# One head group's transposes moved from TensorE to a DMA, and a hold on loads released earlier

## The chip, the cores and the metric

The kernel runs on one core of one Trainium2 chip. The core has five engines that run side by side, each through its own queue in order: TensorE (PE, matrix multiplies; PEld is its loading of weights), VectorE (DVE), ScalarE (ACT), GpSimd (POOL) and SyncE (SP). In this kernel POOL issues the loads, and SP issues DMA transposes and stores. Sixteen DMA engines move the data; the profile calls the queue that POOL feeds q0 and the one that SP feeds q1. The metric is the time of one execution on the device in microseconds.

## The reference

Two steps, in f32 at the interface. The kernel computes in f16 with f32 sums.

```python
scores = scale * np.matmul(q, k.transpose(0, 1, 3, 2)) - np.log(S)
attn = 1.0 / (1.0 + np.exp(-scores))
attn_out = np.matmul(attn, v)
x = attn_out.transpose(0, 2, 1, 3).reshape(B * S, H * D)
out = (np.maximum(x @ w_gate, 0.0) * (x @ w_val)) @ w_out
```

q, k and v are 8 batches x 12 heads x 448 positions x 64 wide. x is 3584 x 768; w_gate and w_val are 768 x 1536, w_out is 1536 x 768. The attention has a sigmoid in place of a softmax, so no sums over rows are needed.

## The kernel before

**Attention.** The 12 heads of a batch are worked on in three head groups of four (`NG = 3`). For a group, q and k have to stand with the head dimension on the partitions: that is the tile `qkT` of (batch, group), which has three buffers. It can be made in two ways. `pe_transposes(b, g, ti)` lets TensorE multiply 14 blocks of k (`ti` 0) or q (`ti` 1) with an identity into a PSUM bank (`trt`, L204), and VectorE copies the bank to `qkT` (L211). `dma_transposes(b, g)` lets VectorE regroup k and q into a tile `rel` with two buffers (L222), and SP issues one DMA that transposes all of it into `qkT` (L226). `both(b, g)` is the two `pe_transposes` of a group. `qk_unit(b, g, c)` then computes the scores of one of seven chunks of keys (L239) and the sigmoid on ScalarE (L187, tile `PT`), and `pv_group(b, g)` multiplies with v (L257) and puts the result into `xT` (L184).

**The gated layer.** Its 1536 columns are 12 chunks f. `gv` computes gate and value of a chunk (L322, tiles `g_ps` and `v_ps`), the relu on ScalarE or VectorE, and their product into `hT` (L343). Batch 0 is split into two halves of its queries (256 and 192), so it has 24 such units, which wait in `gv_queue`. Later batches use a scheme with fewer multiplies on sums of tiles (L400, L714), whose sums VectorE makes (L391, L584), among them sums `T` of the weight `wo`.

**Order.** All of it is one order written out by hand; each engine's queue follows it. Batch 0's attention comes first. Then, for batch 1, six bursts of `qk_unit` (units 0 to 2, 3 to 5, 6 to 8, 9 to 12, 13 to 16, 17 to 20 of the 21 of a batch) alternate with `ffn_mix`, which takes 4, 3, 3, 3, 3 and 4 units from `gv_queue`. `hooks` puts further work into a mix: the pair (3, job) runs the job when 3 units of the mix are left, so with a mix of 3 ahead of them all. Unit 6 is the last of group 0; group 1 begins with unit 7, the second of the third burst.

**Loads.** POOL issues them in the order written, k and q a head group at a time (`load`), w_gate and w_val a few chunks at a time (`load_gv`), v of a batch in three transfers (`load_v`). It has eight completion semaphores for them, so an issue waits for the landing of the one eight places before it. `load(2, ...)` reuses batch 0's tiles. `late_loads`, in the last mix of batch 1, issues the DMA transpose of batch 2's third group and then `hold(2, 2)`: a tiny copy on POOL that reads that `qkT`, and so keeps POOL from issuing v of batch 2, k and q of batch 3, `wo` and v of batch 3 until that transpose has landed.

**PSUM.** After batch 0 eight banks go round in a ring (`bank`); who takes a bank waits for the reader of what it held eight takes earlier.

Of the kernel before, what the change touches and what calls it, by code (L numbers as in the profile page):

```python
# [18 lines left out]
def kernel(  # L19
# [75 lines left out]
    def tiles_of(b):  # L95
        if b not in in_tiles:
            pool = early if b == 1 else inp
            in_tiles[b] = tuple(
                p.tile([P, NPAIR, NCH * D], FP16, tag=t, name=t)
                for p, t in ((pool, "k16"), (pool, "q16"), (vinp, "v16"))  # L100
            )
        return in_tiles[b]

    def rows_of(src, b):
        return src[b].rearrange("(x r) (t c) d -> (r t) x (c d)", r=2, c=NCH)

    def load(b, g0, g1, which, c0=0, c1=NCH):
        for nm, t16, src in zip("kq", tiles_of(b), (k, q)):
            if nm in which:
                xs, cs = slice(2 * g0, 2 * g1), slice(c0 * D, c1 * D)  # L110
                nc.gpsimd.dma_start(t16[:, xs, cs], rows_of(src, b)[:, xs, cs])  # L111

    def load_v(b):
        v16 = tiles_of(b)[2]
        nc.gpsimd.dma_start(v16[:, 0::2, :], rows_of(v, b)[:, 0::2, :])
        for r in range(2):
            nc.gpsimd.dma_start(
                v16[64 - 64 * r : P - 64 * r, 1::2, :], rows_of(v, b)[64 * r : 64 * r + 64, 1::2, :]
            )
# [25 lines left out]
    def load_gv(f0, f1, which=(0, 1)):  # L145
        fs = slice(f0 * P, f1 * P)
        for i in which:
            wt, src = ((wg, moe_w_gate), (wv, moe_w_val))[i]
            nc.gpsimd.dma_start(wt[:, :, fs], src[:, fs].rearrange("(c p) f -> p c f", p=P))  # L149
# [2 lines left out]
    load_gv(0, 2)  # L152
    load_gv(2, 4)
    load(1, 0, 1, "kq")
    load_gv(4, 6)
    load(1, 1, 2, "kq")
    load_gv(6, 9)
    load_v(1)
    load(1, 2, 3, "kq")
# [30 lines left out]
    def qkT_of(b, g):  # L190
        if (b, g) not in qkT_tiles:
            qkT_tiles[(b, g)] = qkTp.tile([P, TW, P], FP16, tag="qkT", name="qkT")
        return qkT_tiles[(b, g)]

    def pe_transposes(b, g, ti, c0=0, c1=NCH):
        transposed(b, g, ti, c0, c1)()
# [21 lines left out]
    def dma_transposes(b, g):  # L218
        k16, q16, _ = in_tiles[b]
        rel = relp.tile([P, TW, P], FP16, tag="rel", name="rel")  # L220
        for ti, t16 in enumerate((k16, q16)):
            nc.vector.tensor_copy(  # L222
                rel[:, ti * NCH : (ti + 1) * NCH, :].rearrange("p c (h d) -> p h c d", h=2),
                t16[:, 2 * g : 2 * g + 2, :].rearrange("p h (c d) -> p h c d", c=NCH),
            )
        nc.sync.dma_start_transpose(  # L226
            qkT_of(b, g)[:], rel[:].rearrange("p c x -> p (c x)")
        )
# [78 lines left out]
    def pv_group(b, g):  # L307
        pv(b, g, 0, S, [PT_tiles.pop((b, g, c))[:, :, 0:S] for c in range(NCH)])
# [453 lines left out]
    def push_gv(b, q0, qn, fs, act_relu=True):  # L762
        for f in fs:
            gv_queue.append(lambda f=f: gv(b, q0, qn, f, act_relu))

    def push_first(half, fs, act_relu=True):
        c0, c1 = HALVES[half]
        push_gv(0, 64 * c0, 64 * (c1 - c0), fs, act_relu)
# [16 lines left out]
    half = QCUT // 2 * D  # L785
# [60 lines left out]
    slots[5].pv()  # L846
    push_first(1, range(0, 4))
    for f0 in range(4, 12, 2):
        for half in range(2):
            for f in range(f0, f0 + 2):  # L850
                push_first(half, (f,), (half, f) not in ((0, 9), (1, 8)))


    order = [(g, c) for g in range(NG) for c in range(NCH)]
# [1 line left out]
    def pv_finish(b):  # L856
        pv_group(b, NG - 1)
# [4 lines left out]
    def hold(b, g):  # L862
        nc.gpsimd.tensor_copy(gate[0:1, :], qkT_tiles[(b, g)][0:1, 0, 0:2])

    def both(b, g):
        pe_transposes(b, g, 0)
        pe_transposes(b, g, 1)

    def late_loads():
        dma_transposes(2, 2)  # L870
        hold(2, 2)
        load_v(2)
        load(3, 0, NG, "kq")
        load_o()
# [57 lines left out]
    for b in range(1, B):  # L932
        if b == 1:
            cuts, pv_at = (0, 3, 6, 9, 13, 17, 21), {3: (0, 2), 5: (1, 2)}
        else:
            cuts, pv_at = (0, 4, 7, 11, 14, 18, 21), {0: (-1, 2), 2: (0, 2), 4: (1, 2)}
        bursts = list(range(len(cuts) - 1))
        inner = {}
        if b > 2:
            inner = {0: 1, 3: 5} if b == 3 else {0: 1} if b % 2 == 0 else {2: 3, 3: 5} if b == B - 1 else {4: 5}  # L940
            for n in inner.values():
                bursts.remove(n)
        count = len(bursts)
        hooks = {}
        if b == 1:
            mix = (4, 3, 3, 3, 3, 4)
            hooks = {
                1: [(3, lambda: both(1, 1))],
                3: [(3, lambda: both(1, 2))],
                4: [(3, lambda: dma_transposes(2, 0)), (1, lambda: dma_transposes(2, 1))],  # L950
                5: [(4, late_loads)],
            }
            steps = itertools.chain.from_iterable(early_sum_steps(j, 2 * j) for j in range(4))
            given = ((0, 0, 1, 1, 1), (0, 1, 1, 0), (0, 1, 1, 1), (0, 1, 1, 0), (2, 0, 0, 0), (0, 1, 1, 1, 1))
        else:
            mix = (0,) * count

        def burst(n):
            for i, (g, c) in enumerate(order[cuts[n] : cuts[n + 1]]):
                if n in pv_at and i == pv_at[n][1]:  # L960
                    if n == 0:
                        pv_finish(b - 1)
                        if b == 2:
                            push_group(0)
                        elif b % 2 == 0:
                            push_group(b // 2 - 1)
                    else:
                        pv_group(b, pv_at[n][0])
                qk_unit(b, g, c)

        for m in range(count):
            jobs, ahead = [], []
            burst(bursts[m])
            if m == 0 and b > 3:
                jobs.append(lambda: dma_transposes(b, 2))
            if b == 2 and m == 2:
                ahead.append(lambda: dma_transposes(3, 0))
            elif b == 2 and m == 3:
                jobs.append(lambda: dma_transposes(3, 1))
            elif b == 3 and m == count - 1:  # L980
                jobs.append(lambda: dma_transposes(4, 1))
            elif 0 <= m - count + 2 and 3 < b < B - 1:
                jobs.append(lambda: dma_transposes(b + 1, m - count + 2))
            if b == 1:
                if m == 0:
                    load(2, 0, 1, "kq")
                    load(2, 1, 2, "kq")
                    load(2, 2, 3, "kq")
            elif m == 0 and b + 1 < B:
                for g0, g1 in ((0, 1), (1, NG)) if b == 3 else ((0, NG),) if b > 3 else ():  # L990
                    jobs.append(lambda g0=g0, g1=g1: load(b + 1, g0, g1, "kq"))
                jobs.append(lambda: load_v(b + 1))
            if b == 2 and m == 0:
                ahead.append(lambda: split_sums(1))
            elif b == 2 and m == 4:
                open_late()
                first_sums = token_sum_steps(0, 0)
                ahead += [*first_sums[:2], lambda: weight_sums(0)]
            elif b == 2 and m == 5:
                ahead += [lambda: weight_sums(1), lambda: dma_transposes(3, 2)]  # L1000
                jobs += first_sums[2:]
            elif b == 3 and m == 0:
                jobs.append(lambda: (weight_sums(2), weight_sums(3)))
            elif b == 3 and m < 3:
                jobs.append(lambda: gate_sums(6 + 2 * m, 8 + 2 * m))
            if b % 2 and b > 2:
                if m == count - 1:
                    jobs.append(lambda: (batch_sums_t1(b // 2), batch_sums(b // 2, (0, 1))))
            elif b > 3 and m == 0:
                jobs.append(lambda: batch_sums(b // 2 - 1, (1, HD)))  # L1010
            if mix[m]:
                for job in jobs:
                    job()
                ffn_mix(mix[m], hooks.get(m, ()), steps, given[m])
            else:
                next_work(
                    jobs, ahead=ahead,
                    amid=(lambda: burst(inner[m])) if m in inner else None,
                )
            if b == 3 and m == count - 2:  # L1020
                dma_transposes(4, 0)
# [35 lines left out]
```

## Time and profile before

| what | value |
|---|---|
| median of 3 runs | 389.93 us (389.64 to 390.08) |
| the profiled execution | 390.18 us |
| its span in the trace | 388.3 us |
| TensorE busy | 381.8 us, 98% |
| VectorE, ScalarE, POOL busy | 300.0, 227.3 and 49.8 us |
| idle stretches of TensorE over 0.2 us after its first 10 us | 0.27 us at 23.56, 0.46 us at 95.07 |
| load queue q0 | 30496 packets, 23.24 MB |
| SP's queue q1 | 37664 packets, 19.24 MB |

Where a row starts with two numbers, they are start and length in microseconds from the start of the span; then come engine, line, operation, the tile written and the tiles read, the shape, and how many instructions the row stands for. In square brackets stands how long the engine was idle before it, and what ended that. In the DMA view a row names a transfer, the queue, how many there were and the time from issue to landing.

Some places in time that the change touches: POOL issued k and q of batch 1's second group at 16.91 and 18.91, and they landed at 30.89 and 32.02; w_gate and w_val of chunks 4 and 5 went out at 14.50 and 15.32. The hold ran at 62.72, the first transfer behind it was issued at 63.20, and the two parts of `wo` landed at 85.42 and 93.11.

### The profile page before, as it was taken

How to read it: one execution, taken by the hardware profiler on the slowest of the kernel's cores; microseconds unless marked ns; L12 is line 12 of the kernel's file. 1: busy time of each engine (PE TensorE's matmuls, PEld its weight loads, DVE VectorE, ACT ScalarE, POOL GpSimd, SP SyncE). 2: the span in 40 equal slices, each digit the busy share in tenths (PEclk: the TensorE clock that was granted, in tenths of full speed). 3: DMA queues.
4: the chain of work that ended last, by engine and by line, in shares of the span. 5: the costliest groups of instructions: out<-in, count | busy, mean ns of one | idle time of the engine just before them, and what ended most of it. 6: DMA issues, size and time to landing. Idle time of an engine off the chain costs nothing.

```text
span 388.3 us, 8972 instructions
## 1 busy us (share of the span) xinstructions
PE 381.8 (98%) x3576; PEld 224.0 (58%) x3576; DVE 300.0 (77%) x595; ACT 227.3 (59%) x480; POOL 49.8 (13%) x73
## 2 busy tenths in 40 slices
PE   8999999999999999999999999999999999999995
PEld 6678776884555545454455554545455555555663
DVE  3455668768777799999757789999987788999553
ACT  5967887567797755555537864545477344333321
POOL 8633305300400300003000300000000000000000
PEclk9999999999999999999999999999999999999999
DMA  9999997999997990227945793222012220000336
GB/s 172 198 200 204 204 205 114 206 194 170 136 247 141 161 224 6 48 49 95 166 89 129 139 233 54 45 52 50 0 38 67 72 72 1 2 0 2 81 82 165
DMA packets 68987, 43.81 MB, mean 113 GB/s; under 512 B 35664, under 2 KB 65616, under 8 KB 68944
## 3 DMA queue, kind: packets, MB, share of 16 engines
q0 software_dynamic: 30496, 23.24, 39.9%
q1 hardware_dynamic: 37664, 19.24, 24.2%
q10 hardware_dynamic: 784, 0.75, 0.6%
q8 instruction: 28, 0.46, 0.5%
q14 instruction: 15, 0.12, 0.1%
HBM read 47.19 MB, written 11.01 MB: 150 GB/s over the span
## 4 chain that ended last, share of the span: by engine, by line
PE 83%; DMA 10%; POOL 3%; issue 1%; DVE 1%; ACT 0%; POOLq 0%; DVEq 0%; ACTq 0%
PE u L400 34%; PE g L400 16%; PE y L400 11%; PE qk_ps L239 7%; PE pv_ps L257 7%; DMA wo<-in_moe_w_out_dram 6%; PE v_ps L322 4%; DMA wv<-in_moe_w_val_dram 3%; PE g_ps L322 3%; PE ya L366 1%; POOL q L111 1%; PE yb L366 1%; PE trt L204 1%; POOL k L111 1%; POOL wg L149 0%
## 5 line engine op out<-in xcount | busy, mean ns | idle before, releaser
L187 ACT ACTIVATE PT<-qk_ps 128x448 f16<-128x448 f32 (+3 forms) x318 | 151.0, 586 | 81.2 <-PE qk_ps L239 80.9
L400 PEld LDWEIGHTS <-S 128*128 128x128 f16 x558 | 54.6, 98 | 44.7
L633 DVE TENSOR_TENSOR gsb<-g,gsb 128x448 f32<-128x448 f32 x72 | 42.8, 624 | 10.1 <-PE g L400 9.5
L239 PE MATMUL qk_ps<-qkT 64*64 64x448 f16 (+2 forms) x756 | 47.4, 336 | 0.5 <-ACT PT L187 0.3
L400 PEld LDWEIGHTS <-hT 128*128 128x128 f16 x306 | 28.5, 98 | 22.7 <-issue 5.2
L629 ACT COPY gsb<-u 128x448 f32<-128x448 f32 x48 | 25.6, 558 | 24.0 <-PE u L400 22.9
L257 PE MATMUL pv_ps<-PT,v 64*64 64x448 f16 (+2 forms) x756 | 36.8, 329 | 0.0
L184 DVE TENSOR_SCALAR xT<-pv_ps 128x448 f16<-128x448 f32 (+2 forms) x53 | 27.8, 566 | 9.9 <-PE pv_ps L257 8.5
L458 ACT ACTIVATE ysb<-u 128x384 f32<-128x384 f32 x30 | 14.7, 490 | 33.9 <-PE u L400 29.0
L400 PEld LDWEIGHTS <-wg 128*128 128x128 f16 x216 | 20.2, 98 | 21.8 <-issue 4.3
L400 PEld LDWEIGHTS <-wv 128*128 128x128 f16 x216 | 21.1, 98 | 19.7
L476 DVE SCALAR_TENSOR_TENSOR ysb<-y,ysb 128x384 f32<-128x384 f32 x29 | 16.1, 556 | 17.9 <-PE y L400 10.8
L239 PEld LDWEIGHTS <-qkT 64*64 64x64 f16 x756 | 17.8, 105 | 20.5 <-issue 14.3
L111 POOL DMA_DIRECT2D k<-in_k_dram x14 | 10.8, 775 | 140.3 <-DVE rel L222 135.2
L257 PEld LDWEIGHTS <-v 64*64 64x64 f16 x756 | 21.8, 107 | 10.9 <-issue 0.9
L400 PE MATMUL u<-T,hT 128*128 128x384 f16 x132 | 25.1, 327 | 0.0
L400 PE MATMUL u<-xT,wg 128*128 128x448 f16 x108 | 23.5, 354 | 0.0
L322 PE MATMUL v_ps<-xT,wv 128*128 128x256 f16 (+2 forms) x168 | 22.8, 273 | 0.7 <-DVE hT L343 0.5
L400 PE MATMUL g<-xT,wg 128*128 128x448 f16 x108 | 23.4, 352 | 0.0
L400 PE MATMUL u<-X,wv 128*128 128x448 f16 x108 | 23.4, 352 | 0.0
L400 PE MATMUL u<-X,S 128*128 128x448 f16 x108 | 23.4, 352 | 0.0
L400 PE MATMUL g<-X,S 128*128 128x448 f16 x108 | 23.4, 352 | 0.0
(94 smaller groups left out, 563.9 us busy)
## 6 DMA issues: line engine op xcount, KB each, us to landing
out_dram<-ysb SPq DMA_DIRECT2D x52, 192.0 KB, 2.9
v<-in_v_dram POOLq DMA_DIRECT2D x8, 336.0 KB, 15.1
v<-in_v_dram POOLq DMA_DIRECT2D x16, 168.0 KB, 14.8
k<-in_k_dram POOLq DMA_DIRECT2D x4, 672.0 KB, 10.9
q<-in_q_dram POOLq DMA_DIRECT2D x4, 672.0 KB, 13.9
k<-in_k_dram POOLq DMA_DIRECT2D x9, 224.0 KB, 12.0
q<-in_q_dram POOLq DMA_DIRECT2D x7, 224.0 KB, 12.3
wo<-in_moe_w_out_dram POOLq DMA_DIRECT2D x1, 1536.0 KB, 18.5
```

Source lines behind the costliest of these rows:

```text
L111: nc.gpsimd.dma_start(t16[:, xs, cs], rows_of(src, b)[:, xs, cs])
L184: nc.vector.tensor_scalar(out=xT, in0=src, scalar1=XSCALE, scalar2=None, op0=AOP.mult)
L187: nc.scalar.activation(PT_ap, ps_ap, AF.Sigmoid, bias=sig_bias, scale=qk_scale)
L239: nc.tensor.matmul(out_of(hh)[o : o + 64, :], qkT[rows, c, cols], qkT[rows, NCH + c0 : NCH + c1, cols], start=True, stop=True, tile_positi ...
L257: nc.tensor.matmul(ps[hh][64 * r : 64 * r + 64, 0:qn], v16[rows, 2 * g + hh, c * D : (c + 1) * D], pieces[c][rows, hh, :], start=(c == 0), ...
L322: nc.tensor.matmul(ps[:, 0:qn], (wg, wv)[i][:, dc, f * P : (f + 1) * P], xT_tiles[b][:, dc, q0 : q0 + qn], start=(dc == 0), stop=(dc == ND ...
L366: nc.tensor.matmul(ps[:, 0 : m1 - m0], hT_tiles[g][:, f, t * P : (t + 1) * P], wo[:, f, m0:m1], start=(f == 0), stop=(f == NFC - 1),)
L400: nc.tensor.matmul(ps[:, 0:n], A[:, k_, :], W[:, k_, :], start=(first and k_ == 0), stop=(k_ == kn - 1), skip_group_check=True,)
L458: nc.scalar.activation(o, ps[:, 0:HM], AF.Copy, scale=OUT_SCALE)
L476: nc.vector.scalar_tensor_tensor(out=o, in0=ps[:, 0:HM], scalar=OUT_SCALE, in1=o, op0=AOP.mult, op1=AOP.add)
L629: by(gs[u][i][:], ps[u][:, 0:S])
L633: nc.vector.tensor_tensor(out=gs[u][i][:], in0=ps[u][:, 0:S], in1=gs[u][i][:], op=AOP.add)
```

## The change

It has four parts. (1) k and q of batch 1's second group are loaded before chunks 4 and 5 of w_gate and w_val instead of after. (2) That group's `qkT` is made by `dma_transposes(1, 1)` ahead of the first mix of batch 1, instead of by TensorE ahead of the second mix. (3) Of the units of chunks 8 to 11, those of chunks 8 and 9 are taken chunk by chunk (8 of both halves, 9 of both) and not half by half; chunks 10 and 11 come as before. (4) POOL's hold in `late_loads` reads `qkT` of batch 2's second group, not of its third.

```diff
     load_gv(2, 4)
     load(1, 0, 1, "kq")
+    load(1, 1, 2, "kq")
     load_gv(4, 6)
-    load(1, 1, 2, "kq")
     load_gv(6, 9)
...
     for f0 in range(4, 12, 2):
-        for half in range(2):
-            for f in range(f0, f0 + 2):
-                push_first(half, (f,), (half, f) not in ((0, 9), (1, 8)))
+        units = [(half, f) for half in range(2) for f in range(f0, f0 + 2)]
+        for half, f in sorted(units, key=lambda u: u[1]) if f0 == 8 else units:
+            push_first(half, (f,), (half, f) not in ((0, 9), (1, 8)))
...
         dma_transposes(2, 2)
-        hold(2, 2)
+        hold(2, 1)
         load_v(2)
...
             hooks = {
-                1: [(3, lambda: both(1, 1))],
+                0: [(4, lambda: dma_transposes(1, 1))],
                 3: [(3, lambda: both(1, 2))],
```

## The prediction

> **What bounds the kernel now.** I read the page first: shares, then the chain.
>
> ```profile
> PE 381.8 (98%) x3576; PEld 224.0 (58%) x3576; DVE 300.0 (77%) x595; ACT 227.3 (59%) x480; POOL 49.8 (13%) x73
> PE 83%; DMA 10%; POOL 3%; issue 1%; DVE 1%; ACT 0%; POOLq 0%; DVEq 0%; ACTq 0%
> DMA  9999997999997990227945793222012220000336
> ```
>
> TensorE is busy for 98% of the span, so a microsecond taken from it is gained, and one in which it waits is lost up to the end: there is no later slack to absorb it. The DMA digits (9.7 us each) show the transfers saturated for the first 58 us; that is where the change works. Next, the timeline of TensorE and VectorE (start, length, operation), around the work that goes and the work that needs its result:
>
> ```profile
> 34.33 0.58 PE L204 MATMUL trt<-ident,k 128*64 128x128 f16 x14
> 34.74 0.56 PE L204 MATMUL trt<-ident,q 128*64 128x128 f16 x14
> ...
> 38.95 0.76 PE L239 MATMUL qk_ps<-qkT 64*64 64x448 f16 x12
> ...
> 93.13 1.36 DVE L391 TENSOR_TENSOR T<-wo 128x2304 f16<-128x2304 f16 x1 [0.95 <-DMA wo<-in_moe_w_out_dram]
> ...
> 95.07 1.29 PE L322 MATMUL v_ps<-xT,wv 128*128 128x448 f16 x6 [0.46 <-DVE hT L343]
> ```
>
> The 28 transposes run from 34.40 to 35.30 on the chain of waits (0.90 us). The burst at 38.95 has three units of four; the first still belongs to group 0, the second, at 39.2, is the first that reads group 1. At 93.13 VectorE waited 0.95 us for wo, and TensorE 0.46 us behind that: its longest idle stretch after the start. Last, the DMA view: what one DMA transpose costs, issue to landing, each in a window around its issue (199.4, 177.5 and 78.4), and under the last the packets of two stretches after that issue (queue, packets, MB):
>
> ```profile
> qkT<-rel SPq DMA_TRANSPOSE x1, 3.9
> ...
> qkT<-rel SPq DMA_TRANSPOSE x1, 10.6
> ...
> qkT<-rel SPq DMA_TRANSPOSE x1, 14.1
> ...
> q0 software_dynamic: 609, 0.62, 124.4%
> ...
> q0 software_dynamic: 949, 0.49, 87.8%
> q1 hardware_dynamic: 947, 0.24, 45.8%
> ```
>
> Idle engines: 3.9 us. With loads issued at the same moment: 10.6. Behind loads already queued: 14.1. From 79 to 82 queue 0 (the loads) moved 609 packets and the transpose none; from 84 to 88 both moved one packet for one (949, 947). A transpose is 128x14x128 f16 in packets of 256 B, 1792 of them, so one for one is slow.
>
> **The change, part by part.** Sums go against the profiled execution (390.18 us; span 388.3 and 1.88 around it). The median of the runs is 389.93, 0.25 less.
>
> *Transposes off TensorE:* -0.90 (above). The two VectorE copies qkT<-trt (618 ns each) go, two rel copies (385 ns) come. They stand behind the xT copies that end at 29.73, in a 2.62 us idle stretch of VectorE ending at 32.34: 0, if their loads are there. Two PSUM banks fewer are taken in the ring, so the next v_ps takes the bank that the hT copy frees at 34.43; TensorE wants it at 35.06: 0.
>
> *Loads sooner:* the load queue lands strictly in order, k or q of one group each 1.12 us after the one before (30.89, 32.02), wg and wv 2.0 us. q of batch 1's first group lands at 25.78 (12.86 + 12.9). So k and q of the second come at 26.9 and 28.0, before the copies at 29.73. wg and wv of chunks 4 and 5 go from 27.78 and 29.77 to 30.0 and 32.0; TensorE wants them at 34.3 and 35.0: 0. POOL issues as many transfers as before; later ones keep their places.
>
> *The DMA transpose:* copies end at 30.42; SP has nothing ahead of it (its next transpose came at 52.04) and issues 0.1 us behind: 30.5. Behind it on SP stands only that next one, and the rel buffer is free again long before the copies at 54.4 want it: 0. TensorE reaches the second unit at 39.2 - 0.9 = 38.3. The latency decides. From below 3.9 (idle engines), from above 15.7 (the transpose issued at 82.83, partly behind another). Nearest is 78.36: then loads for over 10 us were queued, as at 30.5 (the last of them land at 41 and later), while the 10.6 had next to none ahead of it. At 78.36 the first packets came after 3.8 us, and a store issued at 105.95 behind queued loads also took 5.3 us instead of 2.9. From 30 to 34 the load queue moves 1056 packets in 4 us, 264 a microsecond; sharing one for one, by the 4 us above and the 529 and 529 packets from 92 to 95, I count 175 to 195 transpose packets a microsecond here. So 3.3 to 3.8 us until the first packet, 1792 / 185 = 9.7, and 0.4 from the last packet to the landing (62.2 to 62.66 for the third transpose): 13.4 to 13.9, the row 14.1. I take 13.9: it lands at 44.4, and TensorE stands for 6.1 us: +6.1. Ends: none (34.4), or 46.2, +7.9. Behind the waiting multiply on TensorE's queue stands everything; ScalarE and VectorE run dry, DMA gains.
>
> *Loads behind it:* 0.46 MB more at 200 GB/s put them 2.3 us later (v 41.2 to 43.5, k and q of the third group 43.5 to 45.8, wv of chunks 9 to 11 49.3 to 51.6). They are wanted at 43.0, 45.1 and 51.5 plus the stall: 0 while the stall lasts; without it up to 0.65.
>
> *Chunk 8 ahead of 9:* the same matmuls on the same engines, chunk 9 one unit (1 us) later: 0.
>
> *The stall's second price:* TensorE's clock. The table by stretch (busy time and count by engine, PEclk third from the right) at both ends of the trace:
>
> ```profile
> 0.00:5.00 5.00, 3.84 (x26) 3.32 (x28) 0.94 (x3) 1.89 (x3) 4.26 (x11) 1.00 0.62 165
> 384.40:387.00 2.60, 0.00 (x0) 0.00 (x0) 0.34 (x1) 0.00 (x0) 0.00 (x0) 1.00 0.79 222
> 387.00:388.30 1.30, 0.00 (x0) 0.00 (x0) 0.00 (x0) 0.00 (x0) 0.00 (x0) 0.60 0.00 0
> ```
>
> The last matmul ends at 384.4, and within 387.0 to 388.3 the granted clock falls (mean 0.60: 0.5 from about 387.25), 2.9 us on. At the start the clock column has no record yet, but 22 matmuls of 194 columns took 3.74 us, 0.88 ns a column, where a row of six of 448 columns takes 1.14 us, 0.42: half speed for 3.7 us, 1.9 us lost. A wait of 6.1 us is twice what let the clock fall at the end, so I take the start's price: +1.9. Ends: 0, and 2.6 if the slow stretch lasts 5 us. The Trainium skill (TensorE: Matmul & The Clock Gate, What's actually happening) has the clock halved after one idle window of about 3.4 us and back after as long a busy one; that speaks against this change too, and by it the term would be 1.7 and the time 396.4; the trace's tail fell sooner, after 2.9 us.
>
> *hold on the second transpose:* before, (2,1) landed at 59.4 and (2,2) at 62.66, and POOL went on at 62.72. Now v of batch 2, k and q of batch 3 and wo are issued 3.2 us sooner against TensorE's place; the third transpose shares engines with them, but is first read at 88.0, 25 us on: 0. wo lands some 3 us sooner than 93.11, which covers the 0.95 us of VectorE's wait: -0.46. Ends: 0 and -0.46. Late next: nothing; that g and v pair then runs back to back.
>
> Sum: 390.18 - 0.90 + 6.1 + 1.9 - 0.46 = 396.8; less 0.25, 396.6.
>
> **Rivals.**
> *The wait without the clock (394.7):* a clock that stays up through one wait. For: no wait inside the trace shows it. Against: the tail.
> *Half the contention (391.2):* latency 10.4 as at 127.79, landing 40.9, wait 2.6: 390.18 - 1.36 + 2.6 - 0.25. For: four of the eighteen transposes took 9 to 11 us. Against: they were issued together with the first loads, not behind a full queue.
> *No wait (389.2, the other side):* the transpose takes about the 3.9 us of idle engines, landing 34.4; then -0.90 - 0.46 + 0.65 for the later loads. It decides at landing 39.7 (38.3 + 1.36), a latency of 9.2. For: 52.04, queued behind four loads, took 5.8. Against: those four were the last, their stream running out 3 us on; at 30.5 it runs 25 us more. The Trainium skill (DMA: Bandwidth & Descriptors, Latency and other measured facts) gives a DMA transpose 261 GB/s; with that page's fixed 2 us this would be an estimated 3.8 us and the time 389.2; rows under load speak against it.
>
> **How the numbers follow.** Wait and clock 0.64 (395 to 398.8 by latency and clock ends), wait alone 0.14, half the contention 0.11, no wait 0.11. The forecast is the first case's 396.6. Leaving out the last case and the edges of the others, 391.0 to 398.8 holds 8 in 10. About 0.2% (0.8 us) is what can be told from no change: no wait splits into faster 0.05 and same 0.06; slower 0.89.
>
> **What would show it.** In the changed profile: 28 matmuls of L204 gone near 34; an SP transpose at 30.5 landing near 44; a wait of TensorE at L239 on DMA qkT<-rel of 6 us, then a stretch with granted clock 0.5; POOL past its hold 3 us sooner against TensorE; no wait on wo. A landing before 39 makes the prediction wrong.

## The result, and the profile after

The changed kernel takes 399.85 us, the median of 5 runs (398.39 to 400.06), against 389.93 us for the kernel before (389.64 to 390.27, 5 runs). The ratio is 1.0242, with a 95% interval of 1.0229 to 1.0254. Of all the runs told of here one stands apart and is in no number below: a run of the unused transpose with batch 2's transposes later took 563.56 us at a mean granted clock of 0.656, where the others of that kernel took about 393 at 1.0. The forecast of 396.6 us has the right sign, but it is 3.2 us short, and the time lies 1.05 us above the upper edge of its range. The profiled execution took 399.64 us, its span 397.6 us.

Busy time by engine and the granted clock in 40 slices, from the page of the changed kernel:

```profile
PE 383.5 (96%) x3548; PEld 224.7 (57%) x3548; DVE 299.6 (75%) x595; ACT 227.4 (57%) x480; POOL 50.2 (13%) x73
PEclk9999599999999999999999999999999999999999
```

28 matmuls are gone (3548 for 3576), yet TensorE is busy 1.7 us longer and the span is 9.3 us longer. The one slice in which the clock is low says where to look, from about 40 to 50 us. The timeline of TensorE there (start, length, operation, and in brackets the idle time before it with what ended that):

```profile
38.12 0.38 PE L239 MATMUL qk_ps<-qkT 64*64 64x448 f16 x4
46.72 0.96 PE L239 MATMUL qk_ps<-qkT 64*64 64x448 f16 x8 [8.21 <-DMA qkT<-rel]
47.61 1.14 PE L322 MATMUL g_ps<-xT,wg 128*128 128x192 f16 x6
```

The burst of three units breaks off after its first (4 matmuls). TensorE stands for 8.21 us until the DMA has made `qkT` of group 1, and the g_ps work after it takes 1.14 us where the kernel before needed 0.67. The table by stretch (busy time and count of PE, PEld, DVE, ACT and POOL, then the granted clock, the DMA share and GB/s) shows both prices:

```profile
40.90:46.70 5.80, 0.00 (x0) 0.00 (x0) 0.00 (x0) 0.00 (x0) 2.51 (x5) 0.50 1.30 183
46.70:51.10 4.40, 4.38 (x28) 3.16 (x29) 0.82 (x2) 2.15 (x6) 1.27 (x2) 0.50 1.31 204
51.10:55.00 3.90, 3.90 (x62) 2.72 (x60) 1.84 (x5) 2.26 (x6) 0.00 (x0) 1.00 1.27 203
```

In the first stretch no engine but POOL, which issues loads, does anything; in the second TensorE works at clock 0.50; in the third it is at full clock again.

I matched each matmul of the kernel before with the same one after and followed the difference of their start times:

| place (time before) | after minus before | step | forecast |
|---|---|---|---|
| up to 34 us | +0.09 | +0.09, the start phase | 0 |
| matmul behind the transposes that went, 35.23 | -0.83 | -0.92 | -0.90 |
| unit 7 of batch 1, 39.16 | +7.55 | +8.38, the wait | +6.1 |
| end of the slow clock, 53.0 | +9.60 | +2.05, the clock | +1.9 |
| v_ps at 95.07 | +9.03 | -0.57, no wait on wo | -0.46 |
| last matmul, 384.35 | +9.03 | 0 | 0 |

The last matmul thus comes 9.03 us later. The tail of the span behind it and the time around the span grew by 0.23 and 0.19 us; together that is 9.45 of the 9.46 us between the two profiled executions. Every step came with the forecast sign, and one has the wrong size: the wait.

The DMA view of the changed kernel says why. The first line is the transpose (issue to landing, from a window at its issue); then come the packets of both queues from 35 to 37, from 38.2 to 39.0, and from 34.4 to 46.2 us:

```profile
qkT<-rel SPq DMA_TRANSPOSE x1, 16.2
...
q0 software_dynamic: 372, 0.29, 90.1%
q1 hardware_dynamic: 373, 0.10, 35.7%
...
q1 hardware_dynamic: 33, 0.01, 94.5%
q0 software_dynamic: 24, 0.02, 63.8%
...
q0 software_dynamic: 1921, 1.57, 92.0%
q1 hardware_dynamic: 1822, 0.46, 38.8%
```

And the load queue of the kernel before over the same stretch, 34.4 to 46.2 us, with no transpose beside it:

```profile
q0 software_dynamic: 2987, 2.37, 128.2%
```

The transpose was issued at 30.50 us, as forecast, and landed at 46.67: 16.18 us in place of 13.9. Its first packet moved at 34.46, 3.96 us after the issue. Then both queues moved packet for packet (372 and 373 in 2 us), until 46.17. In 38.2 to 39.0, and once more about 43.3 to 43.7, both nearly stood still (33 and 24 packets in 0.8 us, where some 140 each would have gone). The kernel before has such a still stretch too, within the transpose of 78.36 on which the forecast rested. Its packets from 88.8 to 89.6, loads and transpose:

```profile
q0 software_dynamic: 18, 0.01, 31.6%
q1 hardware_dynamic: 21, 0.01, 29.8%
```

While the transpose of the changed kernel moved its 0.46 MB, the loads lost 2.37 - 1.57 = 0.80 MB, 4.0 us of their stream (2.37 MB in 11.8 us is 201 GB/s). That second price is hidden under the wait here, and shows below.

### The profile page after: what moved, and what is told of

It is laid out like the page before. It is cut to its first block, busy times and chain, and to the rows that moved or that the text cites. A ratio compares the mean times of both kernels' runs of the same rounds, so it can differ in the third digit from the quotient of the medians.

```text
span 397.6 us, 8919 instructions
## 1 busy us (share of the span) xinstructions
PE 383.5 (96%) x3548; PEld 224.7 (57%) x3548; DVE 299.6 (75%) x595; ACT 227.4 (57%) x480; POOL 50.2 (13%) x73
## 4 chain that ended last, share of the span: by engine, by line
PE 92%; DMA 4%; ACT 2%; DVE 1%; issue 0%; DVEq 0%; ACTq 0%
PE u L400 33%; PE g L400 15%; PE y L400 10%; PE qk_ps L239 9%; PE pv_ps L257 8%; PE g_ps L322 4%; DMA qkT<-rel 4%; PE v_ps L322 4%; PE u L714 2%; ACT PT L187 2%; PE g L714 2%; PE warm_ps L175 1%; PE ya L366 1%; PE yb L366 1%; PE trt L204 1%
## 5 line engine op out<-in xcount | busy, mean ns | idle before, releaser
L239 PE MATMUL qk_ps<-qkT 64*64 64x448 f16 (+2 forms) x756 | 48.2, 339 | 8.7 <-DMA qkT<-rel 8.2
L257 PE MATMUL pv_ps<-PT,v 64*64 64x448 f16 (+2 forms) x756 | 36.7, 329 | 0.0
L343 DVE TENSOR_TENSOR hT<-gate_sb,v_ps 128x256 f16<-128x256 f32 (+2 forms) x28 | 11.7, 419 | 21.6 <-PE v_ps L322 16.0
L322 PE MATMUL g_ps<-xT,wg 128*128 128x256 f16 (+2 forms) x168 | 24.0, 283 | 0.0
## 6 DMA issues: line engine op xcount, KB each, us to landing
v<-in_v_dram POOLq DMA_DIRECT2D x16, 168.0 KB, 15.7
```

The source lines that it names most:

```text
L239: nc.tensor.matmul(out_of(hh)[o : o + 64, :], qkT[rows, c, cols], qkT[rows, NCH + c0 : NCH + c1, cols], start=True, stop=True, tile_positi ...
L257: nc.tensor.matmul(ps[hh][64 * r : 64 * r + 64, 0:qn], v16[rows, 2 * g + hh, c * D : (c + 1) * D], pieces[c][rows, hh, :], start=(c == 0), ...
L322: nc.tensor.matmul(ps[:, 0:qn], (wg, wv)[i][:, dc, f * P : (f + 1) * P], xT_tiles[b][:, dc, q0 : q0 + qn], start=(dc == 0), stop=(dc == ND ...
L343: nc.vector.tensor_tensor(out=hT_tiles[g][:, f, o : o + qn], in0=gate_sb[:, 0:qn], in1=ps[1][:, 0:qn], op=AOP.mult,)
```

## The experiments

The theory: the whole loss is one wait for a transpose that shares the DMA engines with queued loads, and the clock that falls in the wait; the other three parts of the change are harmless. The rivals: the reordered loads or the earlier hold cost something themselves; the clock is no price of its own; the latency belongs to the transpose and not to its neighbours.

### The hold alone

The kernel before with one line changed.

```diff
-        hold(2, 2)
+        hold(2, 1)
```

> The kernel before with the hold moved alone (POOL released by the second transpose of batch 2). Theory: wo is issued 3 us sooner, VectorE no longer waits for it near 93, and TensorE's wait of 0.46 us near 95 goes: 389.5 us. Rival: the third transpose and the loads now share the engines and something behind it comes late: 389.9 or more, with a new wait of TensorE between 62 and 100.

Measured: 389.53 us (389.23 to 390.39, 11 runs) beside 390.17 for before; ratio 0.9991 (0.9982 to 1.0001). The timeline of TensorE near the place where it waited 0.46 us:

```profile
93.18 1.31 PE L322 MATMUL g_ps<-xT,wg 128*128 128x448 f16 x6
94.33 1.30 PE L322 MATMUL v_ps<-xT,wv 128*128 128x448 f16 x6
```

No bracket any more: the g and v matmuls run back to back. The wait is gone in the trace, as forecast; in the time the gain sits at the edge of what can be told.

### All but the DMA transpose

The changed kernel with group 1's transposes back on TensorE; loads, order and hold stay changed.

```diff
-                0: [(4, lambda: dma_transposes(1, 1))],
+                1: [(3, lambda: both(1, 1))],
```

> The changed kernel with the one group's transposes back on TensorE, at their old place; the three other parts of the change stay. Theory: the order of the loads and of chunks 8 and 9 costs nothing, so it equals the kernel with the hold moved alone: 389.5 us, and the whole loss of 10 us belongs to the DMA transpose. Rival: a part of the loss comes from the loads of chunks 4 and 5 that stand later, or from the order of the chunks: over 390.5 us.

Measured: 389.37 us (389.04 to 390.06, 11 runs); ratio 0.9983 (0.9974 to 0.9992). TensorE has no idle stretch over 0.2 us after the first 20 us, and the clock stays at 1.0 to its last matmul. So the three other parts together cost nothing, and this version is faster than both kernels, by 0.17% over before. All of the loss belongs to the DMA transpose in its place.

### The wait without the clock

The changed kernel with 42 matmuls of zeros, whose result nobody reads, ahead of the unit that waits.

```diff
+                if (b, n, i) == (1, 2, 1):
+                    keep_warm(42)
```

> The changed kernel with 42 multiplies of zeros (448 columns, about 8 us in all) on TensorE just ahead of the unit that waits for the DMA transpose, so that TensorE is busy while it would wait. Theory: the wait itself is unchanged (the transpose lands near 46.7), but the granted clock stays at full speed and the work behind the wait runs at its old pace: 2.1 us less than the changed kernel, 397.7 us. Rival: the slow work behind the wait comes from readers of PSUM banks or late loads and not from the clock: 399.8 us with the same slow stretch.

Measured: 397.26 us (396.78 to 397.90); ratio 1.0188 (1.0172 to 1.0204). The timeline of TensorE:

```profile
38.41 8.12 PE L175 MATMUL warm_ps<-zeros 128*128 128x448 f16 x42
46.76 0.57 PE L239 MATMUL qk_ps<-qkT 64*64 64x448 f16 x8 [0.23 <-DMA qkT<-rel]
```

And the stretch of the zeros in the table (busy time and count by engine, granted clock third from the right):

```profile
38.50:46.70 8.20, 8.03 (x42) 3.93 (x41) 0.60 (x2) 0.98 (x2) 2.84 (x4) 1.00 1.19 172
```

The unit starts at 46.76, as in the changed kernel (46.72), at clock 1.00, and takes 0.57 us instead of 0.96. The ratio falls by 0.0054, 2.1 us of 390 (1.3 to 2.9 by the two intervals): the price of the clock, by taking it away, against 2.05 us in the trace and 1.9 forecast.

### The keys alone by DMA

Half the transpose: the keys' 7 blocks (896 packets) by DMA, the queries by TensorE one mix later.

```diff
-                0: [(4, lambda: dma_transposes(1, 1))],
+                0: [(4, keys_by_dma)],
+                1: [(3, lambda: pe_transposes(1, 1, 1))],
```

> The changed kernel with only the keys of that group through the DMA transpose (half the size, 896 packets) and the queries transposed by TensorE at the old place. Theory (about 4 us behind the queued loads, then one packet for one): 4 + 896 / 165 + 0.5 = 10 us from an issue at 30.2, landing near 40.1; TensorE comes to it at 38.75 and waits 1.4 us, too short for the clock to fall: 389.93 - 0.45 - 0.46 + 1.4 = 390.4 us. Rival: the latency does not depend on the size (a fixed delay of some 16 us behind the queue): landing near 46, a wait of over 7 us, about 399 us.

Measured: 394.23 us (392.57 to 396.14, 4 runs); ratio 1.0111 (1.0078 to 1.0143). My 390.4 was wrong. The transpose in the DMA view (issue to landing):

```profile
qkT<-rel SPq DMA_TRANSPOSE x1, 11.4
```

The wait behind it, on the timeline of TensorE:

```profile
41.84 0.96 PE L239 MATMUL qk_ps<-qkT 64*64 64x448 f16 x8 [2.78 <-DMA qkT<-rel]
```

And the table over the slow stretch:

```profile
41.00:47.80 6.80, 5.96 (x35) 4.28 (x36) 1.12 (x3) 2.46 (x6) 3.59 (x5) 0.50 1.30 202
```

Halving the packets took 4.8 us off the latency (16.2 to 11.4), which is 5.4 us for each 1000 packets, the still stretches counted in, and leaves some 6.5 us that the halving doesn't touch. The wait came out at 2.78 us, 1.4 above what I expected, and it let the clock fall, which I had ruled out. Here the clock costs more than in the changed kernel, although the wait is a third: the slow stretch is 6.83 us, and only 0.83 of it lies under the wait. A slow stretch costs half of the time that TensorE works in it: (6.83 - 0.83) / 2 = 3.0 us here, against (10.24 - 5.84) / 2 = 2.2 in the changed kernel. The spread of the runs fits: the mean granted clock was 0.997 in the fastest and 0.990 in the slowest, which is the profiled one.

### A transpose nobody waits for

The version with TensorE's transposes again, plus the same two `rel` copies and the same DMA transpose at the same time, into a tile that nobody reads before it is loaded anew.

```diff
-                0: [(4, lambda: dma_transposes(1, 1))],
+                0: [(4, unused_transpose)],
+                1: [(3, lambda: both(1, 1))],
```

> The changed kernel with the group's transposes back on TensorE, and the same two VectorE copies and the same DMA transpose issued at the same time into a tile that nobody reads until it is loaded anew (extra work; nothing is left out). It measures the transfer by itself. Theory: the transpose takes 14 to 16 us again and pushes the loads behind it by about 3 us, but TensorE waits only for those loads, by 1.5 us at most: 389.5 to 391 us. Rival: the cost of the change is in the displaced loads or the extra work on VectorE and not in TensorE's wait for the result: well over 392 us.

Measured: 393.95 us (393.83 to 394.30); ratio 1.0098 (1.0080 to 1.0116): 3.8 us lost, although no instruction waits for the transpose. I had expected 391 at most; the rival's time came. The two extra copies on VectorE are not it: up to 43.9 us TensorE keeps within 0.3 us of the version without the transpose. The timeline, TensorE and VectorE:

```profile
45.29 1.51 PE L257 MATMUL pv_ps<-PT,v 64*64 64x448 f16 x25 [0.63 <-DMA v<-in_v_dram]
...
54.52 0.39 DVE L222 COPY rel<-k 128x896 f16<-128x896 f16 x1 [2.39 <-DMA k<-in_k_dram]
55.67 0.39 DVE L222 COPY rel<-q 128x896 f16<-128x896 f16 x1 [0.76 <-DMA q<-in_q_dram]
...
56.92 0.35 DVE L336 TENSOR_SCALAR gate_sb<-g_ps 128x192 f32<-128x192 f32 x1
...
57.32 0.84 PE L239 MATMUL qk_ps<-qkT 64*64 64x448 f16 x4 [1.00 <-DVE gate_sb L336]
```

The same two copies in the version without the transpose:

```profile
50.85 0.39 DVE L222 COPY rel<-k 128x896 f16<-128x896 f16 x1 [0.24 <-DMA k<-in_k_dram]
51.95 0.39 DVE L222 COPY rel<-q 128x896 f16<-128x896 f16 x1 [0.70 <-DMA q<-in_q_dram]
```

The loads behind the transpose land some 4 us later. TensorE then loses about 1.2 us waiting for v of batch 1 itself, and about 2.6 us through VectorE: its two copies for batch 2's first group wait in order for k and q, and the relu of a chunk (`gate_sb`), which is ready to go, stands behind them. So the displaced loads have a price of their own, about 3.8 us, which the wait of the changed kernel hides.

### The transpose with the queue empty

The changed kernel with all loads behind chunks 4 and 5 of w_gate and w_val held until the transpose has landed (the loads of batch 2's k and q, which stand later in the program, are moved along).

```diff
-    load_gv(6, 9)
-    load_v(1)
-    load(1, 2, 3, "kq")
-    load_gv(9, 12)
...
-                0: [(4, lambda: dma_transposes(1, 1))],
+                0: [(4, transpose_then_load)],
```

> The changed kernel with all loads behind chunks 4 and 5 held on POOL until this DMA transpose has landed, so that it runs with the load queue running empty near 31.7. The time is no measure here, since the held loads come 5 to 8 us late. Theory: the latency is contention with queued loads, so it falls to 4 to 5.5 us, landing near 35, and TensorE does not wait at that unit; it waits later, for chunks 6 to 8, some 5 us. Rival: this transpose is slow in itself or for being the first one of the execution: latency of 14 us or more with an empty queue.

Measured: 398.44 us in the one run. The time is not the point; the latency and what came after are. The DMA view:

```profile
qkT<-rel SPq DMA_TRANSPOSE x1, 4.1
```

The timeline of TensorE:

```profile
41.44 0.83 PE L318 MATMUL g_ps<-xT,wg 128*128 128x256 f16 x6 [1.20 <-DMA wg<-in_moe_w_gate_dram]
44.53 1.46 PE L318 MATMUL v_ps<-xT,wv 128*128 128x256 f16 x6 [2.26 <-DMA wv<-in_moe_w_val_dram]
```

The same transpose, issued 0.3 us later, takes 4.1 us instead of 16.2. So 12 of its 16 us are the loads beside it: alone, its first packet came 1.27 us after the issue (3.96 beside the loads), and its 1792 packets took 2.3 us (11.7). TensorE doesn't wait for `qkT` any more, but for weights that are now late, and the clock falls again (0.5 for 6.8 us from 43.35). So in both orders something is late: either the transpose or the weights.

### The unused transpose, batch 2's transposes later

To test the chain through VectorE: the unused transpose again, with the `rel` copies of batch 2's groups moved to later places, so that they don't block the relu.

```diff
-                4: [(3, lambda: dma_transposes(2, 0)), (1, lambda: dma_transposes(2, 1))],
-                5: [(4, late_loads)],
+                4: [(0, lambda: dma_transposes(2, 0))],
+                5: [(4, lambda: dma_transposes(2, 1)), (0, late_loads)],
```

> The kernel with the unused DMA transpose again, but VectorE takes up batch 2's first group only behind the last unit of the fifth mix, the second ahead of the sixth mix and the third behind it, so that nothing of batch 1 stands behind a copy that waits for late loads. Theory: of the 4 us that the unused transpose cost, 2.6 came from VectorE waiting in order for k and q of batch 2, which the transpose had pushed back by 4 us; they go, and only the 1.2 us wait for v stays: 390.5 to 391.3 us. Rival: those 2.6 us come from something else between 52 and 58 (ScalarE, PSUM banks): about 394 us again.

Measured: 393.06 us (393.04 to 393.55, 3 runs), ratio 1.0081 (1.0064 to 1.0098); 391 was expected. Up to the end of batch 1, TensorE loses 0.6 us instead of 3.8: the chain was there and is gone. About 1 us of this is not the chain's: the program is the same up to 47 us, yet v landed at 44.17 here and at 45.24 before, so that TensorE hardly waited for it. But `late_loads` is now later too, and with it `wo`, for which VectorE waits on the timeline, with TensorE behind it:

```profile
95.39 1.36 DVE L391 TENSOR_TENSOR T<-wo 128x2304 f16<-128x2304 f16 x1 [2.40 <-DMA wo<-in_moe_w_out_dram]
...
97.34 1.29 PE L322 MATMUL v_ps<-xT,wv 128*128 128x448 f16 x6 [1.90 <-DVE hT L343]
```

That is the wait of TensorE that the changed hold removes, come back at four times its length. A second version took `late_loads` four units sooner, and kept the rest.

```diff
-                5: [(4, lambda: dma_transposes(2, 1)), (0, late_loads)],
+                5: [(4, lambda: dma_transposes(2, 1)), (4, late_loads)],
```

> As the kernel with the unused transpose and late copies of batch 2, but with the third group's copies and the loads behind the hold at the start of the sixth mix again and not at its end, since that had brought wo late and made a new wait near 97. Theory: up to batch 2 the displaced loads now cost only 0.6 us (the waits for v and for q of the third group), and wo is no longer late: 390.0 to 390.6 us. Rival: VectorE's wait for batch 2's loads comes back at another place, or the 4 us are lost otherwise: 393 us or more.

Measured: 393.54 us (393.06 to 394.17), ratio 1.0089 (1.0072 to 1.0106); the rival's outcome. The wait on `wo` is gone, and a new one stands in front of it, on the timeline of TensorE and VectorE:

```profile
61.92 0.40 DVE L222 COPY rel<-k 128x896 f16<-128x896 f16 x1 [2.42 <-DMA qkT<-rel]
...
63.80 0.38 PE L239 MATMUL qk_ps<-qkT 64*64 64x448 f16 x3 [0.42 <-DVE hT L343]
```

`rel` has two buffers; the third group's copies want the first group's buffer, whose DMA transpose was issued later (57.04) and lands only at 61.80, so VectorE stands for 2.42 us with four products `hT` behind it. Against the version without the transpose, TensorE is 1.4 us later by 47.5 us (v and q of batch 1) and 2.7 us later by 64.5. Three placements, three different waits, 3.2 to 3.8 us lost in each: the copies were in the way sooner (of the loads) and later (of `wo` and `rel`).

### Filling the wait

The changed kernel with five units of batch 0's gated layer moved ahead into the mix in front of the unit that waits (8 of them instead of 3), and 14 matmuls of zeros behind them; the later mixes are shorter for it, and the later transposes and VectorE's sums are placed anew.

```diff
-            mix = (4, 3, 3, 3, 3, 4)
+            mix = (4, 8, 1, 1, 1, 5)
...
+                if (b, n, i) == (1, 2, 1):
+                    keep_warm(14)
```

> The changed kernel, with five more units of batch 0's gated layer moved ahead of the unit that waits (mixes of 4, 8, 1, 1, 1 and 5 units), 14 multiplies of zeros behind them to keep the clock, and batch 2's copies on VectorE as late as in the other kernel of this call. Theory: the wait is empty time that other work can fill: TensorE takes up the unit at 46.7 with 5.6 us of later work already done, so 16.4 us are left up to batch 2 instead of 22.0 and it starts at 63.1, 1.9 later than before: about 391.5 us, and not under the kernel before, since the loads are still 4 us late. Rival: other waits (late weights, ScalarE) take the place of the wait that was filled: 394 us or more.

Measured: 399.44 us (395.26 to 401.09), ratio 1.0230 (1.0155 to 1.0306); 391.5 was expected. The wait at unit 7 is gone, but `late_loads` came at the end of its mix here too, and the profiled run has a wait of 2.17 us on VectorE's hT at 100.75, with the clock at 0.5 for 3.41 us around it. With `late_loads` taken sooner:

```diff
-                5: [(5, lambda: dma_transposes(2, 1)), (0, late_loads)],
+                5: [(5, lambda: dma_transposes(2, 1)), (4, late_loads)],
```

> As the kernel with five units moved into the wait, with the third group's copies and the loads behind the hold near the start of the sixth mix again. In the earlier trace TensorE began batch 2 at 65.14, 4.0 us after the kernel before, and lost 2.2 us and half the clock for 3.4 us behind wo. Theory: only the wait for wo and the clock behind it go: about 4 us slower than before, 393.5 to 394 us, so filling the wait wins back 6 of the 10 us and the late loads and bursts bound by ScalarE keep the rest. Rival: wo comes late again, and the time stays over 396 us.

Measured: 394.21 us (393.53 to 394.52), ratio 1.0104 (1.0086 to 1.0123), close to the 393.5 to 394 expected. The timeline of TensorE:

```profile
40.27 0.83 PE L322 MATMUL v_ps<-xT,wv 128*128 128x256 f16 x6 [0.44 <-DMA wv<-in_moe_w_val_dram]
...
44.64 2.82 PE L175 MATMUL warm_ps<-zeros 128*128 128x448 f16 x14
...
57.18 1.95 PE L257 MATMUL pv_ps<-PT,v 64*64 64x448 f16 x28
```

Real work in front of the wait wins back 5.6 of the 10 us. What stays lost holds 2.8 us of zeros, 0.4 us for a weight that the transpose made late, and bursts with only one unit between them, where a `pv` takes 1.95 us instead of 1.5. In this form too the transpose costs more than the 0.9 us of TensorE that it frees.

## Why the prediction was right or wrong

**Right.** The loss as such and its place: TensorE waits at unit 7 for `qkT`, with everything on its queue behind it. Of the terms, the transposes that go (-0.92, forecast -0.90), the clock (+2.05 in the trace, 2.1 by taking it away, forecast +1.9) and the hold (-0.57, forecast -0.46) were right in size, and so were the loads taken sooner: k and q of group 1 landed at 26.93 and 27.71 us (26.9 and 28.0), and the transpose was issued at 30.50 (30.5). Chunk 8 ahead of 9 cost nothing: the version with everything but the DMA transpose shows no new wait. That the clock's size came out so near is in part luck: it was taken from the start of the trace, and the half transpose shows 3.0 us behind a wait a third as long.

**The step that failed: the latency.** The forecast was 13.9 us, with 15.7 as its upper end; it measured 16.18, and the wait 8.21 us in place of 6.1. Three pieces: the first packet came after 3.96 us, where I took 3.3 to 3.8. The 1792 packets took 11.7 us, where I took 9.7; outside the still stretches the rate was about 170 to 175 a microsecond, below the 185 I used, and the two still stretches, for which the sum has no term, took 1.3 us together. One was there to be seen: I counted packets from 84 to 88 and from 92 to 95, on either side of the one at 88.8. The landing came 0.5 us behind the last packet, as taken. I had drawn the upper end at the longest row of the trace, but none of those rows lay beside a stream of loads as long as this one (25 us more, by the prediction's own count), so the longest of them was no upper bound. The range was also drawn too low by its own ends: 390.18 - 0.90 + 7.9 + 2.6 - 0.46 - 0.25 = 399.1, not 398.8. The wait of 8.38 against 6.1 is 2.3 of the 2.8 us by which the sum was short; most of the rest, 0.4, is the longer tail and the time outside the span.

**A step priced wrongly, and hidden by the wait.** "Loads behind it" had 2.3 us later, from 0.46 MB at 200 GB/s, and at most 0.65 us without the stall. They came 3.8 to 3.9 us later (wv of chunks 9 to 11 landed at 53.09 instead of 49.30, k and q of batch 2's first group by 55.40 instead of 51.53), and 4.1 if one counts the 0.3 us by which the loads had been ahead at 34.6. Two things made it more than the bytes. The queues moved packet for packet, and a packet of the loads holds some 0.8 KB, one of the transpose 256 B: by the prediction's own rates (264 load packets a microsecond alone, 185 beside the transpose, for 9.7 us, 760 B each) that is 0.58 MB, 2.9 us. And in the 1.3 us of still stretches the loads stood too, moving 0.03 MB where 0.26 would have gone: 1.1 us more. With nothing waiting for the transpose, the price was 3.2 to 3.8 us in the three placements tried, through v of batch 1 and VectorE's order. So the rival "no wait" at 389.2 could hold only for a transpose that is short as well: one of 16 us that nobody waits for gave 393.95, 0.9 us of it TensorE's own transposes. The Trainium skill (DMA: Bandwidth & Descriptors, Queues, rings and completion order) has each DMA engine take turns between queues packet by packet, and the counts (372 and 373) agree. A packet, as the Trainium skill has it there, holds several descriptors (single pieces of a transfer); whether that is what the profile counts as a packet, no run here shows.

**The rivals.** "The wait without the clock" is refuted: the trace has the clock at 0.5 for 10.24 us, and keeping TensorE busy returned 2.1 us. "Half the contention" didn't happen, and its 391.2 was too low as well: the experiment with half the packets had about its wait (2.78 us for 2.6), and measured 394.23, since such a wait also lets the clock fall (3.0 us in the profiled run, where TensorE loses nothing more behind it).

**Open.** Why both queues stand still within the transpose is not settled. Each still stretch of the changed kernel began about 1 us after a small instruction transfer (16 KB at 37.2 us, 8 KB at 42.3), and so did the one of the kernel before (16 KB at 87.84, still from 88.8). In every other trace with the transpose beside loads in this place one lies between 37.7 and 39.4 too, about 1 us behind such a 16 KB transfer. An 8 KB one at 36.8 left none, nor did those beside loads alone (36.7 and 47.2 in the kernel before). That is a coincidence in time and was not tested.

## What to carry to other kernels

Before moving work from the bounding engine to a DMA, look at what the DMA engines do at that time: a transpose in small packets that takes 4 us on an empty queue took 16 beside a full one, and it cost the loads 0.80 MB for its own 0.46. Price the transfer for those behind it even when its own result is not urgent, and follow each delayed load into engines that run in order, where it blocks work that is ready. And a wait of 2 to 3 us on TensorE can be dearer than its length, when the clock falls and stays down over the work that follows.

## What the runs showed of the hardware that I had not expected

The granted clock falls after less idle time than I took from the trace's tail (2.9 us). It fell 1.95 us into a wait (from 39.05, down at 41.00, the half transpose), 1.97 us into another (from 98.58, down at 100.55, the first version of the filled wait), 2.38 us into the long one (38.50, down at 40.88), and after two waits that made 2.3 of the last 3.4 us idle (the transpose with the queue empty, down at 43.35); a single wait of 1.90 us that ended at 97.34 left it up.

The slow stretches lasted 3.41, 6.83 and 10.24 us: one, two and three times 3.41. The fast ones between two changes are whole multiples of it too (34.13, 95.57, 344.75 and 382.29 us: 10, 28, 101 and 112 times). So in these traces the clock changes at the edges of a grid of 3.41 us that lies elsewhere in each execution, and the same wait costs more or less by where it falls. Behind the last matmul the fall came 2.5 us later in one trace (the changed kernel) and 5.2 in another (the unused transpose with batch 2's transposes later), so the tail's 2.9 us was no threshold.

The Trainium skill (TensorE: Matmul & The Clock Gate, What's actually happening) has windows of that length, and the lengths agree; but it has the clock fall after an idle window, and in the window of 3.41 us that ended at 41.00 TensorE had still worked for 1.46 us. So a window that is 57% idle was enough here; the wait of 1.90 us that left the clock up lay in one window too, from 95.12 to 98.54 (counted in steps of 3.413 us from 6.38, where that trace's clock came up), and made 56% of it.
